# Later due times for DMAs in a planner, a wider gate, and two more DMA transposes, in a recurrence followed by a feed-forward stage

## The chip, the cores and the metric

The kernel runs on one core of a Trainium2 chip. The metric is device time in microseconds (us) of one execution. Three executions of the kernel before were timed: 184.87, 186.39 and 186.94 us, median 186.39 us. A fourth one was profiled, and all readings of the trace are from it.

## The reference

```python
# q, k, v, alpha: (B=4, H=8, S=768, D=48) float32; w_in 384x2048, w_out 2048x384
for t in range(S):
    state = alpha[:, :, t, :, None] * state + einsum('bhd,bhe->bhde', k[:, :, t], v[:, :, t])
    y[:, :, t] = einsum('bhd,bhde->bhe', q[:, :, t], state)
x = y.transpose(0, 2, 1, 3).reshape(B * S, H * D)        # 3072 tokens of 384
out = (relu(x @ w_in) ** 2) @ w_out                      # 3072 x 384
```

A gated linear recurrence (the "GLA part") makes x, and a feed-forward stage (the "MoE part", in the kernel's names m1 for `x @ w_in` and m2 for the product with `w_out`) makes the output from it.

## The kernel before, in words

The 3072 tokens are cut into 24 chunks of 128 tokens, numbered 0 to 23, six to a batch entry. A chunk passes through the GLA part like this. Four loads of 192 KB (`at` for alpha, `qt`, `kt`, `vt`; `add_load`, issued at L371 on SyncE's queue) bring it in. ScalarE takes the logarithm of alpha (L396, tile `L_s`); TensorE sums the logarithms over the tokens (`p0`, and `pT` in transposed form); ScalarE exponentiates the sums. From chunk 11 on (`RAW`) q and k are cast to bf16 on GpSimd (L413, tile `rawb`) and transposed by DMA (L416, tile `rawt`, two per chunk), and VectorE multiplies them with the transposed exponentials (L507 for q, L510 for k, both into tile `qkT`). TensorE makes the scores (tile `sc`), VectorE masks them (L561), TensorE adds both parts of y, and ScalarE casts y to bf16 (L386, tile `xn`). Last, xn is transposed into `xT_big`, the right operand of m1. Before the change, chunks 18 to 22 do this by a DMA transpose on SyncE's queue (L620); the others by three TensorE transposes (issued by a helper, so their line is L243) into a PSUM bank and a copy on VectorE (L388).

The MoE part takes the chunks in 12 groups: group 0 is chunks 0 to 3, groups 1 and 2 are one chunk each, and groups 3 to 11 two each (group 7 is chunks 14 and 15, group 8 is 16 and 17, group 9 is 18 and 19). m1 of a group needs x of all its chunks. It writes three PSUM banks in turn; ScalarE applies the relu out of them (L676, tile `r`), VectorE squares (L684, tile `gT`), and m2 of the group follows. All matmuls are issued by one helper, so they share line L240 and are told apart by their tiles.

The order of the work is made by a planner in the kernel's own Python (`Plan`, `Op`). Every operation is added with an engine, an estimated duration, an added latency `lat` until its result may be used, and a priority. `run` plays the program through on paper, engine by engine, and sorts all operations by their planned start; they are emitted in that order, and each engine and DMA queue of the chip then works through its own list in order, waiting where a semaphore says so. A planned figure therefore costs no time by itself: it moves an operation up or down in the list of its engine. The lists that matter here:

- "DMA" (loads) and "TR" (DMA transposes) both end up in SyncE's one queue. A load has duration `LD1` = 1.0 and `lat` 2.4 from chunk 6 on, so its data are planned for 3.4 us after its planned start. A transpose of q or k has duration `TLD` = 1.0 and `lat` `TLAT` = 4.0, so 5.0 us, and its place in the list is set 2.0 us later (`TLATE`, through the field `late`). The DMA transpose of xn has 0.8 + 4.0 us and `late` 1.0.
- A gate holds back TensorE's first operation of a chunk in the GLA part: chunk s may start when s <= LEAD + (MoE work planned so far) / 5.12, where a chunk's MoE work is 5.12 planned us, and LEAD is 3.7.

```python
            op.start = t + getattr(op, "late", 0.0)
            ...
            op.done = t + op.dur + op.lat
            ...
        self.order.sort(key=lambda o: o.start)
```

Of the kernel before, what the change touches and what calls it, by code (L numbers as in the profile page):

```python
# [141 lines left out]
def kernel(  # L142
# [93 lines left out]
    def pin(ins):  # L236
        tc.keep_in_program_order(ins)
# [4 lines left out]
    def tr(*a):  # L242
        pin(nc.tensor.transpose(*a))  # L243
# [14 lines left out]
    X_SLACK = 0.2  # L258
    LD = 0.98
    LD1 = 1.0  # L260
    WLD = 2.1
    LAG = 3.2
    SQ_PRIO = 0.0

    def add(eng, dur, emit, *deps, **kw):
        return plan.add(Op(eng, dur, emit, deps, **kw))
# [6 lines left out]
    def load_w(which):  # L273
# [25 lines left out]
        prev = w_cast[-SB] if len(w_cast) >= SB else None  # L299
        ld = add("DMA", WLD * n / 4 + 0.03, e_issue, prev, lat=LAG if which == "o" else 2.0)  # L300
        op = add({"POOL": 0.1 + 0.46 * n, "DVE": 0.1 + 0.2 * n, "ACT": 0.1 + 0.32 * n}, 0, e_cast, ld, prio=-3.0)
# [8 lines left out]
    SRC = dict(srcs)  # L310
    EARLY = 4
    RAW = 11
    XTURN = (18, 23)
    TLD, TLAT, TLATE = 1.0, 4.0, 2.0
    NR = 3
    R = {}

# [46 lines left out]
    def add_load(s, nm):  # L364
        d = C[s]
        b, c = divmod(s, NCH)

        def ld():
            if nm not in d:
                d[nm] = loads.tile([P, H, D], FP32, name=nm)  # L370
            pin(nc.sync.dma_start(out=d[nm], in_=SRC[nm][b, c]))  # L371
        prev = C[s - LB].get("use_" + nm) if s >= LB else None
        d["ld_" + nm] = add("DMA", LD if s < 4 else LD1, ld, prev, lat=2.0 if s < 4 else LAG if s < 6 else 2.4, at=0.6)

    def add_chunk(s):
        d = C[s]
# [189 lines left out]
        if not last:  # L566
# [7 lines left out]
            prev = C[s - 1].get("sb") if s else None  # L574
            if c == 0 and s:
                prev = C[s - 2]["sb"]
# [37 lines left out]
        def e_p4():  # L614
            d["px"] = psum(p4, [P, KT, P], BF16)
            for j in range(KT):
                tr(d["px"][:, j, :], d["xn"][:, j * P:(j + 1) * P], ident_bf)
        if XTURN[0] <= s < XTURN[1]:
            def e_xt():
                pin(nc.sync.dma_start_transpose(out=xT_big[:, :, s * P:(s + 1) * P], in_=d["xn"]))  # L620
            d["x"] = add("TR", 0.8, e_xt, xn, lat=TLAT)
            d["x"].late = 1.0
            d["end"] = xn
            return
        p4 = plan.add(Op("PE", 0.165, e_p4, [xn], takes=GLA_BANKS, lat=0.14, **g))
# [159 lines left out]
    for d in DMA_ORDER + list(range(6, NT)):  # L785
        if d in ("i", "o"):
            load_w(d)
        elif d == "at":
            add_joint_alpha()
        elif isinstance(d, tuple):  # L790
            add_load(*d)
            if d[0] >= JN:
                if all("ld_" + nm in C[d[0]] for nm, _ in srcs):
                    add_chunk(d[0])
            elif d == JLAST:
                for s in range(JN):
                    add_chunk(s)
        else:
            for nm, _ in srcs:
                if nm != "at":  # L800
                    add_load(d, nm)
                elif d <= 9:
                    add_load(d, nm)
                if nm == "at" and 9 <= d < NT - 1:
                    add_load(d + 1, nm)
            add_chunk(d)
# [24 lines left out]
                b2 = add_last(g, tt, b2, pools) if GT[g] + tt == NT - 1 else add_moe2(g, tt, b2, {}, range(NQ), pools)  # L831
        sq[(g, "free")] = b2

    LEAD = 3.7

    def gate(op):
        s = getattr(op, "gla", None)
        if s is not None:
            return s <= LEAD + (prog["m1"] + prog["m2"]) / 5.12
        return True  # L840
# [60 lines left out]
```

## Time and profile before

| What | Value |
|---|---|
| median of three runs (lowest, highest) | 186.39 us (184.87, 186.94) |
| the profiled execution: its own time | 185.07 us |
| its span, from the first to the last instruction | 183.4 us |
| mean granted TensorE clock | 1.000 |
| busy: PE (TensorE) | 177.5 us, 97% of the span |
| busy: DVE (VectorE), ACT (ScalarE), POOL (GpSimd) | 127.1, 126.5, 39.4 us |
| DMA issues on SyncE's queue that are transposes | 26 of q and k, 5 of x |
| share of the 16 DMA engines taken by SyncE's queue (q1) | 80.7% |

PE is the matmul side of TensorE and PEld its weight loads, which overlap with it. A busy PE counts each matmul from its start to its end; matmuls are pipelined, so a second may start before the first has ended, and 97% busy is not 97% of what TensorE could do. The chain of waits follows the program back from its last instruction, at every step to what released it. SPq is SyncE's queue, which issues loads and DMA transposes and waits for nothing but their semaphores.

### The profile page before, as it was taken

Reading aid. Unit: us, or ns where it says so; the run is one execution under the profiler, and the core shown is the slowest. Engines: PE = TensorE matmul, PEld = TensorE weight load, DVE = VectorE, ACT = ScalarE, POOL = GpSimd, SP = SyncE. Lnnn points to the kernel's source line nnn. Section 1 sums busy time; section 2 is a strip of 40 time slices with the busy share of each in tenths; the row PEclk is TensorE's granted clock in tenths of the full one; section 3 lists DMA queues with packets and bytes.
Section 4 is the critical chain, followed back from the end, with each engine's and each line's share of the span. In section 5 each row is a group of like instructions: output and inputs, shape, how many; then the busy total and the mean of one; then the engine's idle time right before and its main releaser. Section 6 shows DMA issues by size and latency. Waiting matters only on the chain.

```text
span 183.4 us, 4946 instructions
## 1 busy us (share of the span) xinstructions
PE 177.5 (97%) x1908; PEld 130.5 (71%) x1908; DVE 127.1 (69%) x273; ACT 126.5 (69%) x286; POOL 39.4 (21%) x80
## 2 busy tenths in 40 slices
PE   7999999899999999999999998999999999999993
PEld 2577884567769877867768776667766777778663
DVE  1179898684999998778877867748855984744200
ACT  3677799226859996966967859847975895767321
POOL 8221100021131142132223133342323512000000
PEclk9999999999999999999999999999999999999999
DMA  5999999999999999998999599898898898901022
GB/s 168 215 212 252 302 366 321 326 220 204 177 191 201 194 179 173 141 190 161 150 193 202 113 240 186 161 227 162 170 201 182 176 163 194 301 13 43 12 77 86
DMA packets 120200, 34.12 MB, mean 186 GB/s; under 512 B 112400, under 2 KB 118928, under 8 KB 120176
## 3 DMA queue, kind: packets, MB, share of 16 engines
q1 hardware_dynamic: 119536, 31.83, 80.7%
q0 software_dynamic: 640, 1.97, 3.2%
q8 instruction: 15, 0.25, 0.6%
q14 instruction: 9, 0.07, 0.2%
HBM read 25.17 MB, written 4.72 MB: 163 GB/s over the span
## 4 chain that ended last, share of the span: by engine, by line
PE 49%; DMA 2%; ACT 1%; issue 0%; DVE 0%
PE bank L240 45%; DMA at<-in_alpha_dram 2%; PE sc L240 2%; PE st L240 1%; PE bank L243 1%; ACT aiT L454 0%; ACT r L676 0%; ACT ob L758 0%; ACT L_s L396 0%; ACT ob L716 0%; DVE xT_big L388 0%; ACT qkT L451 0%
## 5 line engine op out<-in xcount | busy, mean ns | idle before, releaser
L240 PE MATMUL bank<-xT_big,w_in_b 128*128 128x256 bf16 (+2 forms) x636 | 76.6, 262 | 0.9 <-ACT r L676 0.7
L240 PE MATMUL bank<-w_out_b,gT 128*128 128x384 bf16 (+1 forms) x400 | 71.6, 320 | 0.5 <-DVE w_out_b L296 0.5
L676 ACT ACTIVATE r<-bank 128x512 bf16<-128x512 f32 x96 | 56.6, 606 | 11.3 <-PE bank L240 9.9
L240 PEld LDWEIGHTS <-w_in_b 128*128 128x128 bf16 x636 | 52.7, 98 | 10.6 <-issue 1.5
L240 PEld LDWEIGHTS <-gT 128*128 128x128 bf16 x416 | 37.2, 98 | 18.7 <-DVE w_out_b L296 1.0
L684 DVE TENSOR_TENSOR gT<-r 128x512 bf16<-128x512 bf16 x96 | 41.8, 453 | 10.2 <-ACT r L676 9.0
L561 DVE TENSOR_TENSOR sm<-sc,utri_b 128x512 bf16<-128x512 f32 x48 | 30.8, 684 | 5.9 <-PE sc L240 5.7
L405 POOL CAST vb<-vt 128x384 bf16<-128x384 f32 x24 | 13.6, 569 | 69.1 <-DMA vt<-in_v_dram 55.2
L386 ACT CAST xn<-bank 128x384 bf16<-128x384 f32 x24 | 11.6, 482 | 11.6 <-PE bank L240 11.5
L505 DVE TENSOR_TENSOR kI_s<-kt,Ainv 128x384 bf16<-128x384 f32 x21 | 12.8, 611 | 7.8 <-ACT Ainv L466 7.8
L240 PEld LDWEIGHTS <-qkT 64*128 64x128 bf16 (+1 forms) x272 | 10.7, 95 | 6.4 <-issue 2.4
L586 ACT CAST sb<-st 128x384 bf16<-128x384 f32 x20 | 9.6, 482 | 7.7 <-DVE st L581 7.5
L758 ACT COPY ob<-bank 128x384 f32<-128x384 f32 x14 | 6.7, 480 | 8.0 <-PE bank L240 8.0
L396 ACT ACTIVATE L_s<-at 128x384 bf16<-128x384 f32 x20 | 10.5, 527 | 2.4 <-DMA at<-in_alpha_dram 2.3
L240 PE MATMUL bank<-warm 128*128 128x256 bf16 (+1 forms) x54 | 10.9, 348 | 1.3 <-DVE warm L188 1.3
L502 DVE TENSOR_TENSOR qA_s<-qt,A 128x384 bf16<-128x384 f32 x11 | 6.3, 575 | 8.0 <-ACT A L462 8.0
L413 POOL CAST rawb<-qt 128x384 bf16<-128x384 f32 x13 | 7.4, 570 | 20.3 <-DMA qt<-in_q_dram 20.3
L413 POOL CAST rawb<-kt 128x384 bf16<-128x384 f32 x13 | 7.6, 587 | 19.0 <-DMA kt<-in_k_dram 11.1
L581 DVE TENSOR_TENSOR st<-st,ae_s 128x384 f32<-128x384 f32 x20 | 11.1, 556 | 0.5 <-PE st L240 0.5
L466 ACT ACTIVATE Ainv<-bank 128x384 bf16<-128x384 f32 x21 | 10.5, 501 | 1.1 <-PE bank L240 1.0
L240 PE MATMUL sc<-qkT 64*128 64x128 bf16 x192 | 9.5, 219 | 0.0
L240 PEld LDWEIGHTS <-sm 128*128 128x128 bf16 x192 | 8.1, 96 | 1.7 <-issue 0.2
(64 smaller groups left out, 165.7 us busy)
## 6 DMA issues: line engine op xcount, KB each, us to landing
qt<-in_q_dram SPq DMA_DIRECT2D x24, 192.0 KB, 4.0
kt<-in_k_dram SPq DMA_DIRECT2D x24, 192.0 KB, 3.6
vt<-in_v_dram SPq DMA_DIRECT2D x24, 192.0 KB, 3.8
at<-in_alpha_dram SPq DMA_DIRECT2D x20, 192.0 KB, 4.0
wo<-in_moe_w_out_dram SPq DMA_DIRECT2D x4, 768.0 KB, 8.5
out_dram<-ob POOLq DMA_DIRECT2D x10, 192.0 KB, 3.1
wi<-in_moe_w_in_dram SPq DMA_DIRECT2D x4, 384.0 KB, 5.3
wi<-in_moe_w_in_dram SPq DMA_DIRECT2D x2, 768.0 KB, 8.3
```

The lines of the kernel that those rows point to most:

```text
L240: pin(nc.tensor.matmul(*a, **kw))
L386: pin(nc.scalar.copy(out_t, in_t))
L396: pin(nc.scalar.activation(L[:, :, 0:D], d["at"], AF.Ln))
L405: pin(nc.gpsimd.tensor_copy(d["vb"], d["vt"]))
L413: pin(nc.gpsimd.tensor_copy(R["b"][:, w, j, :, 0:D], d[nm]))
L466: pin(nc.scalar.activation(d["Ai"], d["pm"][:, 0:HD].rearrange("p (h d) -> p h d", h=H), AF.Exp, scale=-1.0))
L505: pin(nc.vector.tensor_mul(kI[:, :, 0:D], d["kt"], d["Ai"]))
L561: pin(nc.vector.tensor_mul(d["sm"][:, hh], d["sc"][:, hh], utri_b.to_broadcast([P, NP, P])))
L581: pin(nc.vector.tensor_mul(st4, st4, bcast(ae, D)))
L586: pin(nc.scalar.copy(d["sbt"], d["st"]))
L676: pin(nc.scalar.activation(box["r"][:, 0:w], box["ph"][:, 0:w], AF.Relu))
L684: pin(nc.vector.tensor_mul(gT[g][:, f0:f0 + per, lo * P:lo * P + n], r, r))
```

## The change

```diff
     LD1 = 1.0
+    LT = 4.2
     WLD = 2.1
...
-    XTURN = (18, 23)
-    TLD, TLAT, TLATE = 1.0, 4.0, 2.0
+    XTURN = (16, 23)
+    TLD, TLAT, TLATE, XLATE = 1.0, 6.0, 2.0, 2.6
...
-        d["ld_" + nm] = add("DMA", LD if s < 4 else LD1, ld, prev, lat=2.0 if s < 4 else LAG if s < 6 else 2.4, at=0.6)
+        d["ld_" + nm] = add("DMA", LD if s < 4 else LD1, ld, prev, lat=2.0 if s < 4 else LAG if s < 6 else 2.4 if s < RAW else LT + (1.0 if nm == "at" else 0.0), at=0.6)
...
-            d["x"].late = 1.0
+            d["x"].late = XLATE
...
-    LEAD = 3.7
+    LEAD = 4.1
```

In words: (1) loads of chunks 11 to 23 are planned to land 5.2 us after their planned start (`at`: 6.2) and not 3.4; (2) DMA transposes of q, k and x are planned to take 2 us longer; (3) the DMA transposes of x get a place in the list that is 1.6 us later than before; (4) chunks 16 and 17 use the DMA transpose for x as well, so their six TensorE transposes and two VectorE copies are gone; (5) the gate lets each chunk's GLA part begin 0.4 chunks of MoE work, 2.05 planned us, earlier. No instruction's size or operands change.

## The prediction

> **What bounds the kernel now.** I read the page first: its busy times and its slices.
>
> ```profile
> PE 177.5 (97%) x1908; PEld 130.5 (71%) x1908; DVE 127.1 (69%) x273; ACT 126.5 (69%) x286; POOL 39.4 (21%) x80
> ...
> DMA  5999999999999999998999599898898898901022
> ```
>
> TensorE is the bound, and in every slice up to 162 us the DMA engines are nearly as full. Next, the table of stretches says where TensorE has anything to give back.
>
> ```profile
> 57.00:104.00 47.00, 46.92 (x546) 36.76 (x543) 39.90 (x87) 38.53 (x91) 11.96 (x21) 1.00 0.94 170
> 104.00:112.00 8.00, 7.33 (x76) 5.32 (x75) 5.22 (x13) 5.48 (x13) 3.05 (x6) 1.00 1.00 208
> 112.00:163.00 51.00, 51.00 (x530) 37.59 (x529) 36.18 (x76) 38.10 (x88) 13.83 (x24) 1.00 0.86 186
> ```
>
> The columns are the stretch, its length, busy PE, PEld, DVE, ACT, POOL, the clock, the DMA share and GB/s. The figures of the change concern chunks 9 and later, so nothing moves before about 57 us; behind 163 us only m1 and m2 are left. Between them PE idles 0.08 + 0.67 + 0 us. One place holds nearly all of it, and the chain of waits names it:
>
> ```profile
> 105.28 4.13 DMA at<-in_alpha_dram
> 109.40 0.02 issue
> 109.42 0.34 ACT L_s L396
> ...
> 111.30 0.49 ACT r L676
> 111.79 0.04 issue
> 111.84 0.49 PE bank L240 x3
> ```
>
> The alpha load of chunk 19 takes 4.13 us where the planner allowed 3.4. ScalarE waits for it in order (0.71 us idle ahead of L_s), with an eviction, two exponentials and a relu queued behind; TensorE has filled its three m1 banks and waits for that relu. TensorE's own timeline gives the size:
>
> ```profile
> 108.89 2.29 PE L240 MATMUL bank<-xT_big,w_in_b 128*128 128x256 bf16 x18
> 111.84 0.49 PE L240 MATMUL bank<-xT_big,w_in_b 128*128 128x256 bf16 x3 [0.66 <-ACT r L676]
> ```
>
> Of such matmuls twelve in a row took 1.47 us with the last counted at its full 0.27, so one starts every (1.47 - 0.27) / 11 = 0.109 us. Eighteen need 1.96; the next group began 2.95 after the first. Lost: 0.99 us, 0.66 of it visible as idle.
>
> **Part 1, two chunks' x by DMA.** Gone are 2 x 3 TensorE transposes. The chain counts three of them in a row at 0.17 us (102.06, 162.04), so 0.34 us, all on the bounding engine. Gone too are two VectorE copies of 0.346 us; DVE is at 69%, so I count 0. Added are two issues on SyncE at 1.21 us (2.5 with the gaps) and their transfers (landing 2.3 to 5.2 us from issue, median 2.5). Loads behind them, those of chunks 20 and 21, come up to 2.5 us later; chunk 20's transposed k has lain 6.5 us before use and chunk 21's 4.8, so 0 here, and 0 to 0.4 us if parts 2 and 5 use that up as well. How late x comes is seen here (chunk 17, then chunk 18):
>
> ```profile
> 122.03 0.48 ACT L386 CAST xn<-bank 128x384 bf16<-128x384 f32 x1 [2.28 <-PE bank L240]
> ...
> 122.96 0.33 PE L243 MATMUL bank<-ident_bf,xn 128*128 128x128 bf16 x3
> ...
> 123.70 0.34 DVE L388 COPY xT_big<-bank 128x384 bf16<-128x384 bf16 x1
> ...
> 124.42 0.82 PE L240 MATMUL bank<-xT_big,w_in_b 128*128 128x256 bf16 x6
> ...
> 128.10 0.50 ACT L386 CAST xn<-bank 128x384 bf16<-128x384 f32 x1
> ...
> 130.92 1.21 SPq L620 DMA_TRANSPOSE xT_big<-xn  x1
> ```
>
> By TensorE, x of chunk 17 is there 2.0 us after its cast began (124.04 - 122.03), and m1 of group 8 starts 0.4 us later. By DMA, the five chunks 18 to 22 took 5.6 to 6.0 us from the cast's start to landing (128.10 to 133.87 the first). So x of group 8 comes 3.7 us later. What hides it: at 124.42 half of tile 13's m2 and all of tiles 14 and 15 are still to do, 40 matmuls at 0.161 us (eight took 1.46, the last of them 0.33) = 6.4 us, besides the GLA work between them. Cost 0 while that cover lasts; without it, up to 3.7 us.
>
> **Part 2, XLATE 2.6.** An x transpose stands 1.6 us lower on SyncE's list, behind one or two more issues (0.57 us a load, 1.2 to 1.9 a transpose). SyncE's own waits say what this is worth:
>
> ```profile
> SPq L416 <- POOL rawb L413: 11.1, 10, 1.7
> ...
> SPq L620 <- ACT r L676: 2.5, 1, 2.5
> SPq L620 <- ACT ob L758: 2.1, 2, 1.2
> ...
> SPq L620 <- ACT ae_s L458: 1.5, 2, 1.0
> ```
>
> (waiter, released by, us, times, longest). With L620 SyncE stood 6.1 us waiting for ScalarE while loads queued behind; the loads can take that time, x of a chunk pays 0 to 1.9 us. TensorE: between -0.2 and 0, I take 0.
>
> **Part 3, loads 1.8 us (alpha 2.8) later on paper.** Their readers move down the lists: L_s on ScalarE, the casts on GpSimd. Seen from issue, loads land after 2.9 to 5.3 us (median 3.6) in this stretch: the old 3.4 was short for half of them, 5.2 for hardly any. L_s of chunk 19 then stands 2.8 us lower, behind the relus that TensorE waited for, and its load has landed. Its first reader, p0 of chunk 19, ran at 128.17, 18 us later, so nothing is late in its place. Gain: the 0.99 us; bounds 0 (another in-order wait takes over) and 0.99 plus the other PE losses I find by spacing after 57 us, about 1 in pieces under 0.25. I take 0.99. GpSimd's 31.4 us of waiting for q and k loads only moves: POOL is busy 21%, and the output DMAs in its list (0.55 us each) have buffers for six.
>
> **Part 4, TLAT 6.** Transposes of q and k are planned for 7.0 us after their cast, not 5.0. In the trace the landing of chunks 12 to 18 came 4.5 to 7.6 us after the cast's end. VectorE's products and the scores move down TensorE's list. PEld waited for L510 six times, 1.6 us in all, behind running matmuls; between -0.4 and 0 on PE, I take 0.
>
> **Part 5, LEAD 4.1.** I counted the w_in and w_out matmuls ahead of each p0 in TensorE's order: 8.38 chunks' worth for chunk 12, 12.38 for chunk 16, 16.38 for chunk 20, against gates of 8.3, 12.3 and 16.3. So p0 sits on its gate, and the gate now opens 0.4 chunks earlier: at 6.77 us a chunk (scores of chunk 11 at 77.30, of chunk 23 at 158.54) that is 2.7 us. No work is added. It pays for part 1's later x (3.7 + up to 1.9 against 2.7) and for the later places of parts 3 and 4. Its price is slack at the transposed k: from its landing to L510 that reads it were 2.7 us at the least (chunk 14) and 6.5 at the most (chunks 19 and 20).
>
> **Sum.** 185.07 - 0.34 - 0.99 = 183.74 us against the profiled execution's own time, which is its span of 183.4 and 1.67 around it. The median of the three runs is 186.39, 1.32 above that execution. No trace shows where a 186.39 run spends it, so I leave it in: 186.39 - 1.33 = 185.06, forecast 185.1 us.
>
> **Rivals.** (B) Nothing but the 0.34 comes: the wait of chunk 19's load moves to another place, as ScalarE and SyncE still work in order and the DMA share at 104 to 112 us was 1.00. For it: L_s waited four times (2.3 us in all), and only once did TensorE feel it, so the place decides. Against: all loads from chunk 11 on get the allowance. 186.39 - 0.34 = 186.05 us.
>
> (C) More comes: the three runs spread over 2.07 us, more than all PE idle after 57 us, and if their excess is also late loads the change removes it. For it: four of the 13 alpha loads came late even in a quick run; against: nothing shown. 185.07 - 1.33 = 183.74 us, a time for the median too.
>
> (D) Slower: the transposed k becomes the wait. Consumers move up 2.7 us (part 5) while transposes slip behind two more loads (2 x 0.64 = 1.3, with the gaps). Chunk 14 has 2.7 us, so its scores would stand 1.3 us in TensorE's list; chunks 11 and 12 (3.0 and 2.8) likewise. A PE stall delays all later readers, so the largest counts, not the sum: 1.3, and 1.9 if three loads go ahead. It decides where the forward move plus the slip pass 2.7 us. Against it: the planner also holds the readers back to 7.0 us after the cast and only one landing in the list above was beyond that. 186.39 - 0.34 + 1.9 = 187.95 us with chunk 19's loss staying.
>
> (E) Slower: x of group 8 comes too late and m2 runs out. It needs x later by more than 6.4 us of m2 plus the GLA work; 3.7 + 1.9 - 2.7 = 2.9 is expected, so it takes 3.5 us more, as one x transpose whose transfer took 5.2 and not 2.5 us (chunk 22) shows to be possible only in part. Were the cover gone, 2.9 us: 186.39 + 2.9 - 0.34 = 188.95 us. By the Trainium skill, "VectorE: DVE Perf Modes", "Rules for kernel authors", a 128x128 transpose belongs on TensorE when PSUM can take the result, with DMA as the other choice; the trace agrees on the delay (2.0 against 5.6 to 6.0 us), but whether that delay reaches TensorE is what (E) decides.
>
> **How the numbers follow.** Forecast 0.44 (own range 184.2 to 185.8), B 0.23, C 0.16, D 0.11, E 0.06. The range leaves out the lower part of C and the ends of D and E: 183.5 to 187.9 us. About 1% (1.9 us) is what a measurement of this kernel can tell from no change, so the lines are at 184.5 and 188.3. Faster by over 1%: C, and about 0.16 of the forecast's lower end, 0.32. Slower by over 1%: E, and 0.07 for the upper end of D, together 0.13. Within: 0.55.
>
> **What would show it.** Right: chunk 19's L_s with no wait that TensorE feels, PE idle between 57 and 163 us under 0.4 us, 51 transposes of xn on L243 instead of 57, seven on L620; p0 of chunk 12 near 77.6 us; m1 of group 8 1 to 3 us later than 124.42 with no idle before it. Wrong: PE or PEld waiting on VectorE's L507 or L510 by more than 0.5 us at once (D), PE idle just ahead of group 8's m1 (E), or ScalarE's wait for an alpha load back at another chunk with TensorE idle behind it (B).

## The result and the profile after

The changed kernel is slower by 0.64%: the ratio to before is 1.0064, 95% interval 1.0035 to 1.0094. Over 22 runs of each, the medians are 186.25 us (184.79 to 189.01) and 185.70 us (183.61 to 187.79). Ratios, here and below, leave out runs more than 1.5% above the fastest of their kernel; medians have all runs, and where the two disagree both are given. The profiled execution of the changed kernel took 185.48 us with a span of 183.6 us, against 185.07 and 183.4 before. Both lie below their kernel's median, so the two traces show where time moved and not the whole difference.

The page of the changed kernel, the same lines:

```profile
PE 176.9 (96%) x1902; PEld 130.2 (71%) x1902; DVE 126.2 (69%) x269; ACT 126.5 (69%) x288; POOL 40.1 (22%) x80
...
DMA  5999899999999989989899898896898898920112
```

and its table of stretches:

```profile
57.00:104.00 47.00, 47.00 (x561) 37.26 (x559) 40.03 (x88) 39.08 (x94) 13.27 (x22) 1.00 0.96 178
104.00:112.00 8.00, 7.33 (x84) 5.54 (x83) 6.93 (x14) 5.87 (x16) 2.64 (x5) 1.00 1.04 210
112.00:163.00 51.00, 50.39 (x498) 36.32 (x497) 31.75 (x65) 35.69 (x83) 13.87 (x24) 1.00 0.86 187
```

Six TensorE instructions are gone, and PE idles 1.28 us between 57 and 163 us where it idled 0.75. Two of the prediction's signs came: p0 of chunk 12 runs at 77.38 us (80.28 before, 77.6 forecast), and m1 of group 8 starts at 127.38, 3.0 us later than before, with no idle time ahead of it. The alpha wait is gone as well, but two others stand in its place. TensorE's timeline at 108 and at 141 us:

```profile
107.93 0.33 PE L240 MATMUL st<-vb,kI_s 128*128 128x96 bf16 x4
108.93 0.40 PE L240 MATMUL sc<-qkT 64*128 64x128 bf16 x8 [0.67 <-DVE qkT L511]
...
140.00 0.81 PE L240 MATMUL bank<-w_out_b,gT 128*128 128x384 bf16 x4
141.43 0.81 PE L240 MATMUL bank<-xT_big,w_in_b 128*128 128x256 bf16 x6 [0.61 <-DMA xT_big<-xn]
```

First the scores of chunk 16 wait for the product with the transposed k (L511 here; lines after the first edit are one higher); then m1 of group 9 waits for x of chunk 19 by DMA. The first of these is not what the change costs: the kernel without x by DMA (below), which is level with before, has the same wait (0.67 us at 109.17). ScalarE's wait for alpha before (who, for whom, us, times, longest), and the tile view of alpha after:

```profile
ACT L_s L396 <- DMA at<-in_alpha_dram: 2.3, 4, 0.7
```

```profile
L397 ACT ACTIVATE L_s<-at x15: 514/522/546, 58.0 to 140.0; 128x384 bf16<-128x384 f32 x15
L372 SPq DMA_DIRECT2D at<-in_alpha_dram x13: 371/576/926, 58.2 to 134.3; - x13
its engine sat idle before it (us, times) until:
who waited for it (us, times):
```

Nothing is listed under "sat idle before it": ScalarE's 2.3 us of waiting for alpha are gone. The x transposes, five before and seven after:

```profile
L620 SPq DMA_TRANSPOSE xT_big<-xn x5: 1206/1210/1966, 130.9 to 155.1; - x5
...
DMA to landing us min/median/max: 2.3/2.5/5.2
```

```profile
L621 SPq DMA_TRANSPOSE xT_big<-xn x7: 1201/1811/2708, 115.5 to 155.5; - x7
...
DMA to landing us min/median/max: 2.3/4.0/5.8
```

An x transpose takes 4.0 us at the median from issue to landing, where it took 2.5, and its issue holds SyncE for 1.81 us and not 1.21. (With x by DMA alone, below, the landing takes 4.0 us too, but the issue stays at 1.21.)

### The profile page after: what moved, and what is told of

The parts are those of the page before. It is cut to its first block, busy times and chain, and to the rows that moved or that the text cites. A ratio compares the mean times of both kernels' runs of the same rounds, so it can differ in the third digit from the quotient of the medians.

```text
span 183.6 us, 4935 instructions
## 1 busy us (share of the span) xinstructions
PE 176.9 (96%) x1902; PEld 130.2 (71%) x1902; DVE 126.2 (69%) x269; ACT 126.5 (69%) x288; POOL 40.1 (22%) x80
## 4 chain that ended last, share of the span: by engine, by line
PE 79%; DMA 8%; ACT 6%; DVE 4%; issue 1%; ACTq 0%; DVEq 0%; SPq 0%
PE bank L240 70%; DMA wi<-in_moe_w_in_dram 5%; PE bank L243 4%; PE sc L240 4%; ACT r L677 4%; DMA xT_big<-xn 3%; PE st L240 1%; DVE qkT L508 1%; DVE sm L562 1%; ACT Ainv L467 1%; DVE gT L685 1%; DVE w_in_b L297 1%; DVE w_out_b L297 0%; ACT xn L387 0%; ACT qkT L452 0%
## 5 line engine op out<-in xcount | busy, mean ns | idle before, releaser
L240 PE MATMUL bank<-xT_big,w_in_b 128*128 128x256 bf16 (+2 forms) x636 | 75.2, 262 | 0.7 <-DMA xT_big<-xn 0.6
L685 DVE TENSOR_TENSOR gT<-r 128x512 bf16<-128x512 bf16 x96 | 41.1, 444 | 15.8 <-ACT r L677 14.8
L414 POOL CAST rawb<-kt 128x384 bf16<-128x384 f32 x13 | 8.2, 634 | 11.9 <-DMA kt<-in_k_dram 11.9
L773 POOL DMA_DIRECT2D out_dram<-ob x10 | 5.6, 556 | 19.6 <-ACT ob L759 14.9
```

What stands on the lines that cost most here:

```text
L240: pin(nc.tensor.matmul(*a, **kw))
L414: pin(nc.gpsimd.tensor_copy(R["b"][:, w, j, :, 0:D], d[nm]))
L685: pin(nc.vector.tensor_mul(gT[g][:, f0:f0 + per, lo * P:lo * P + n], r, r))
```

## The experiments

Theory X: x of chunks 16 and 17 by DMA is the loss, either because x comes late (X-late) or because two more transposes load SyncE's queue and the DMA engines (X-load). Theory L: the wider gate is the loss. Theory P: the later planned landings and places are.

| kernel | ratio to before, 95% interval | median us (before's beside it) |
|---|---|---|
| whole change | 1.0064 (1.0035 to 1.0094) | 186.25 (185.70) |
| x by DMA alone | 1.0058 (1.0010 to 1.0106) | 186.71 (185.87) |
| whole without x by DMA | 1.0007 (0.9967 to 1.0047) | 185.53 (185.87) |
| LEAD alone | 1.0088 (1.0048 to 1.0129) | 187.25 (185.87) |
| whole without LEAD | 1.0117 (1.0032 to 1.0201) | 189.39 (185.87) |
| alpha's landing alone | 1.0023 (0.9980 to 1.0066) | 185.46 (185.85) |
| later landings and places alone | 1.0021 (0.9988 to 1.0053) | 186.06 (185.85) |
| no x by DMA at all | 1.0050 (1.0011 to 1.0089) | 186.51 (185.85) |
| two transposes into scratch, planned | 1.0136 (1.0074 to 1.0198) | 188.81 (185.85) |
| x planned late, on TensorE | 1.0033 (0.9990 to 1.0077) | 186.14 (185.91) |
| x by DMA moved to other chunks | 1.0045 (1.0003 to 1.0086) | 186.46 (185.91) |
| alpha's landing and LEAD 3.9 | 1.0078 (1.0041 to 1.0116) | 187.14 (185.91) |
| x by DMA alone, group 9 later | 0.9993 (0.9929 to 1.0057) | 187.21 (185.93) |
| whole, group 9 later | 1.0101 (1.0034 to 1.0167) | 187.35 (185.93) |
| alpha's landing, group 9 later | 1.0003 (0.9960 to 1.0045) | 185.42 (185.93) |
| two transposes into scratch, outside the plan | 1.0064 (1.0019 to 1.0109) | 187.40 (185.83) |
| five of them | 1.0300 (1.0223 to 1.0376) | 192.74 (185.83) |

**Part by part.** Each of x and LEAD was done alone and left out.

```diff
 # x by DMA alone, on the kernel before         # whole without x: XTURN = (18, 23)
-    XTURN = (18, 23)
+    XTURN = (16, 23)
 # LEAD alone, on the kernel before             # whole without LEAD: LEAD = 3.7
-    LEAD = 3.7
+    LEAD = 4.1
```

> The kernel before with one edit: x of chunks 16 and 17 by DMA (XTURN 16). The whole change measured 1.0064 of before, about +1.2 us. Theory X (the two chunks' x by DMA lands 3.7 us later, loads SyncE's queue, and m1 of groups 8 and 9 waits for it): about +1.2 us, ratio 1.004 to 1.008. Theory L (the wider gate puts readers of DMA data too early in TensorE's order): -0.3 us, the six transposes gone, ratio 0.998. Theory P (the later planned landings and places push x back): -0.3 us as well.

> The changed kernel with x of chunks 16 and 17 back on TensorE (XTURN 18). Theory X: the loss is gone, 1.000 of before or a little less. Theories L and P: the loss stays, ratio 1.006 to 1.009 (the 0.34 us of transposes come back on top).

> The kernel before with LEAD 4.1 alone. Theory L: +1.2 us, ratio 1.005 to 1.008, with TensorE waiting on VectorE's product with the transposed k (L511) in the trace. Theories X and P: no loss, 0.997 to 1.002; by the prediction's reading a little less than before, since a wider gate pays for late data.

> The changed kernel with LEAD back at 3.7. Theory L: the loss is gone, ratio 0.998 to 1.002. Theory X: the loss grows, since the gate no longer pays for the later x: 1.008 to 1.02. Theory P: it grows too, 1.008 to 1.02. If the parts are independent and small, 1.006.

X by DMA costs 0.58% alone, and without it the rest of the change stands level with before: theory X holds both ways. LEAD costs 0.88% alone, yet taking it out of the whole does not bring the time back: theory L holds for the old landings and falls for the new ones. (Whether the whole is worse without LEAD is not shown: the median is 3.1 us higher, but the two intervals overlap.) ScalarE's wait for alpha with LEAD alone:

```profile
ACT L_s L397 <- DMA at<-in_alpha_dram: 8.6, 8, 2.2
```

ScalarE waits 8.6 us for alpha where before it waited 2.3, as chunks are asked for earlier and alpha is still planned too soon. TensorE idles 2.99 us between 57 and 163 us in that execution (188.88 us, above that kernel's median), and its two longest waits, 0.86 us at 73.22 and 1.18 us at 113.10, follow back along the chain to an alpha load. It is not the whole of LEAD's cost: with alpha's landing planned later and a gate of 3.9 the kernel still measures 1.0078 (below).

**Landings alone, no x by DMA, scratch.** One edit sets alpha's `lat` to 5.2 for chunks 11 to 23 and nothing else; one sets LT, TLAT and XLATE alone; one sets `XTURN = (23, 23)`; one adds, to the kernel before, planned DMA transposes into a tile that nobody reads:

```diff
+        if s in (16, 17):
+            def e_sx():
+                pin(nc.sync.dma_start_transpose(out=scr[:, :, (s - 16) * P:(s - 15) * P], in_=d["xn"]))
+            add("TR", 0.8, e_sx, xn, lat=TLAT).late = XLATE
```

> The kernel before with one edit: alpha's loads of chunks 11 to 23 are planned to land 6.2 us after their start. Theory A (the prediction's part 3: ScalarE's in-order wait for alpha is what TensorE lost): ScalarE's wait for alpha falls from 2.3 us to about 0 and the time by up to 1 us, ratio 0.994 to 0.998. Rival (another in-order wait takes over at once): the wait falls too, the time stays, 0.998 to 1.003.

> The later planned landings and places alone (LT, TLAT, XLATE), with LEAD 3.7 and x of chunks 16 and 17 on TensorE. If the parts add up (whole change 1.006, without the lead 1.012, x about 0.006): 1.004 to 1.008, with TensorE waiting in front of m1 for x that the plan puts later. If the later landings are free and only x cost in the run without the lead: 0.997 to 1.002.

> The kernel before with no x by DMA at all: chunks 18 to 22 go back to TensorE, 15 transposes more, 0.85 us of TensorE by the prediction's price. If x by DMA costs more than it saves for every chunk, as theory X-load has it: faster than before, 0.985 to 0.998. If only the place matters (X-late; before has no wait for these five): slower by the 0.85 us, 1.003 to 1.007.

> The kernel before, with x of chunks 16 and 17 still transposed on TensorE, and a DMA transpose of the same two xn tiles into a scratch tile besides, which nobody reads (extra work, not less). Theory X-load (the two transposes cost by loading SyncE's queue and the DMA engines): about the loss of the first experiment, ratio 1.004 to 1.009. Theory X-late (they cost because m1 waits for x that comes later): 0.998 to 1.003.

> A second profile of the two transposes into scratch. If its loss is the edit's: again 187 us or more and TensorE waiting for a transposed k near 153 us. If the wait there was an accident: a loss spread over other places.

With alpha's landing alone, ScalarE's wait fell from 2.3 to 0.3 us and no gain could be measured; in its trace TensorE idles 0.69 us elsewhere, ahead of group 9:

```profile
142.10 0.50 PE L240 MATMUL bank<-xT_big,w_in_b 128*128 128x256 bf16 x3 [0.69 <-DMA xT_big<-xn]
```

All landings and places together, without LEAD and x, are level too. Without any x by DMA the kernel is slower by 0.5%, near the 0.85 us priced for 15 transposes: for chunks 18 to 22 the DMA path pays, so X-load is not true of every chunk. The planned scratch run measures more than x by DMA itself, though the intervals overlap. (In the scratch kernels line numbers are two to four higher than before.) In its first profile TensorE waited 2.58 us at 155.7 us for L512, the product with the transposed k of chunk 22, which had landed 0.1 us before the product began; in the trace of before this k lay 5.0 us. The second profile took 186.05 us and had this wait at the same place:

```profile
150.24 1.46 PE L241 MATMUL bank<-w_out_b,gT 128*128 128x384 bf16 x8
152.38 0.40 PE L241 MATMUL sc<-qkT 64*128 64x128 bf16 x8 [0.68 <-DVE qkT L512]
```

So the wait comes with the edit, and its length changes from execution to execution.

**Late or load.** The second profile of x by DMA alone (185.76 us), at group 9 again:

```profile
139.97 0.36 PE L240 MATMUL bank<-vb,sm 128*128 128x48 bf16 x8
141.34 0.50 PE L240 MATMUL bank<-xT_big,w_in_b 128*128 128x256 bf16 x3 [1.00 <-DMA xT_big<-xn]
```

```diff
 # x planned late, on TensorE: XWAIT = 4.1 planned us behind the copy's duration, 3.7 later than before
-            deps = [C[s]["x"] for s in ...]
+            deps = [(C[s]["x"], XWAIT if s in (16, 17) else None) for s in ...]
 # x by DMA moved
-        if XTURN[0] <= s < XTURN[1]:
+        if s in (16, 17, 20, 21, 22):
 # group 9 later: on x by DMA alone, on the whole change, on alpha's landing alone
-            d["x"] = add("TR", 0.8, e_xt, xn, lat=TLAT)
+            d["x"] = add("TR", 0.8, e_xt, xn, lat=TLAT + (1.5 if s in (18, 19) else 0.0))
```

> A second profile of x of chunks 16 and 17 by DMA alone. If the wait ahead of m1 of group 9 is what the edit costs, it is there again with about 1 us of idle TensorE; if it was one execution's accident, the lost time sits elsewhere in this profile.

> The kernel before with one edit in the planner: m1 may use x of chunks 16 and 17 only 3.7 planned us later than it is there, about what the DMA path costs on paper. x stays on TensorE, no DMA is added. Theory X-late (the order with a later m1 of group 8 is what costs): the loss of x by DMA without its saving, 1.006 to 1.009. Theory X-load (the two more transposes in SyncE's queue and on the DMA engines cost): no loss, 0.997 to 1.002.

> The kernel before with five x by DMA as before, but of chunks 16, 17, 20, 21 and 22, and those of 18 and 19 on TensorE. Theory X-load by count: as many DMA transposes as before, so 0.997 to 1.003. X-load by place (a transpose costs where loads of four more chunks still come behind it): 1.003 to 1.008. X-late at group 9 (TensorE waits only for x of chunk 19): no wait for x ahead of group 9, 0.996 to 1.001.

> The kernel before with alpha planned to land 6.2 us after its start and LEAD 3.9, no other part of the change. If the wider gate hurts alone only because alpha then comes late: 0.993 to 1.000, a candidate faster than both kernels. If the wider gate costs by other waits too: 1.002 to 1.008.

> x of chunks 16 and 17 by DMA alone, with x of chunks 18 and 19 planned to land 1.5 us later, so that m2 work stands ahead of m1 of group 9. If the wait ahead of group 9 is the loss (1.0058): no such wait in the trace, about 1 us less, ratio 0.998 to 1.002. If the two transposes cost by load on SyncE's queue and the DMA engines: the wait goes but the loss stays, 1.004 to 1.008.

> The whole change with the same edit: x of chunks 18 and 19 planned 1.5 us later still. If the wait ahead of group 9 (0.61 us idle in its profile) is the loss: 1.000 to 1.004. If load is: 1.005 to 1.008.

> Alpha planned to land 6.2 us after its start, LEAD 3.7, x of chunks 16 and 17 on TensorE, and x of chunks 18 and 19 planned 1.5 us later. Its predecessor without the last edit had 0.69 us idle ahead of group 9 and a median of 185.46 us. If both in-order waits are the loss that can be had back: 0.992 to 0.998, faster than both kernels. If the waits move again: 0.998 to 1.003.

The wait ahead of group 9 repeats (1.07 and 1.00 us): x of chunk 19 took 5.1 and 5.2 us from issue to landing, where it took 2.4 before. Planned away, the wait goes, and the loss does not: in the whole change the ratio stays at 1.0101, and the trace (of an execution of 189.41 us) has 1.9 us of TensorE waiting for L511 in three places instead. On x by DMA alone that edit is undecided (ratio 0.9993, but the median is 1.3 us above before's). x planned late is undecided as well (1.0033 lies between both theories), and moving two of the five DMA transposes to earlier chunks measures 1.0045, as X-load by place has it, with an interval (from 1.0003) that does not exclude X-load by count. Alpha's landing with a gate of 3.9 was to be a faster kernel and is not: x of chunk 19 was waited for 1.84 us. Alpha's landing with the old gate and group 9 later was to be faster as well and is level. No version is shown to beat the kernel before.

The last two runs took the planner out. They issue the transposes into scratch from inside the emission of the VectorE copy, so the lists of the compute engines are those of before (in the traces these engines run the same instructions in the same order, and SyncE's list differs by the added issues alone):

```diff
             cast(xT, xT_big[:, :, s * P:(s + 1) * P], d["px"])
+            if 16 <= s < 18:      # the second run: 13 <= s < 18
+                pin(nc.sync.dma_start_transpose(out=scr[...], in_=d["xn"]))
```

> The kernel before, its order on TensorE, VectorE, ScalarE and GpSimd unchanged, with two DMA transposes of xn into a scratch tile (chunks 16 and 17) on SyncE's queue that no plan knows of: extra work, nothing left out. Theory load: 1.004 to 1.009, with TensorE waiting for a transposed k or an x behind them. Theory order (what costs is that the planner reshuffles everything): 0.998 to 1.003.

> The same with five such transposes, of chunks 13 to 17. Theory load: two and a half times the first run's loss, 1.010 to 1.025. Theory order: 0.998 to 1.005.

Theory order falls, X-load stands: 1.0064 for two, 1.0300 for five, which is more than load was expected to cost (1.010 to 1.025). The first one's trace is of an execution of 188.93 us, above that kernel's median. TensorE waits 0.73 us for the scores of chunk 20. The product named there, L512, needs the transposed k, but this k had landed at 133.09, 6.5 us before L512 began. The chain of waits leads to another load, alpha of chunk 23:

```profile
134.01 3.64 DMA at<-in_alpha_dram
...
138.56 0.51 ACT qkT L453
...
139.09 0.43 DVE qkT L509
...
139.60 0.44 DVE qkT L512
140.04 0.05 issue
140.09 0.40 PE sc L241 x8
```

ScalarE waits for this alpha in order, with the exponentials of chunk 20 (L453) queued behind it. It already did so in the trace of before; the first line is from there, the second from the run with two transposes outside the plan:

```profile
136.42 0.52 ACT L396 ACTIVATE L_s<-at 128x384 bf16<-128x384 f32 x1 [0.46 <-DMA at<-in_alpha_dram]
...
137.67 0.52 ACT L398 ACTIVATE L_s<-at 128x384 bf16<-128x384 f32 x1 [1.26 <-DMA at<-in_alpha_dram]
```

ScalarE's wait is 0.80 us longer. The second wait of TensorE is for x of chunk 21, issued at 155.08 where before issued it at 151.71:

```profile
157.78 0.49 PE L241 MATMUL bank<-xT_big,w_in_b 128*128 128x256 bf16 x3 [2.13 <-DMA xT_big<-xn]
```

SyncE's list has hardly a gap, and an added transpose (1.21 and 1.79 us) takes the place of two or three loads:

```profile
117.18 0.58 SPq L373 DMA_DIRECT2D kt<-in_k_dram  x1
117.85 1.21 SPq L632 DMA_TRANSPOSE scr<-xn  x1
119.11 0.57 SPq L373 DMA_DIRECT2D vt<-in_v_dram  x1
119.74 0.57 SPq L373 DMA_DIRECT2D at<-in_alpha_dram  x1
120.35 0.89 SPq L373 DMA_DIRECT2D qt<-in_q_dram  x1
```

Just behind the second one the list stood 2.8 us behind that of before. A part of this was made up, but alpha of chunk 23 was still issued 1.21 us late (first line before, second line this run), while TensorE was only 0.45 us late (scores of chunk 19 at 132.40 and 131.95):

```profile
132.80 0.58 SPq L371 DMA_DIRECT2D at<-in_alpha_dram  x1
...
134.01 0.68 SPq L373 DMA_DIRECT2D at<-in_alpha_dram  x1
```

With five transposes the same load stops TensorE at the same scores. It is issued at 135.52 and lands at 140.66, while the transposed k of these scores had landed at 134.76:

```profile
140.69 0.52 ACT L398 ACTIVATE L_s<-at 128x384 bf16<-128x384 f32 x1 [3.94 <-DMA at<-in_alpha_dram]
...
143.27 0.61 PE L241 MATMUL sc<-qkT 64*128 64x128 bf16 x8 [3.57 <-DVE qkT L512]
```

## Why the prediction was wrong, point by point

- **Part 1 failed, by its load.** The prediction priced the two transposes' load on what stands behind them at 0, with 0 to 0.4 us as the bound, because the transposed k of chunks 20 and 21 had 6.5 and 4.8 us of slack. Two transposes outside the plan cost 1.0064, about 1.2 us at 185.83; x by DMA alone cost 1.0058, 1.1 us, with the 0.34 us of TensorE saved inside it. The slack was read for the transposed k alone, but the same list carries the alpha loads and x. Alpha of chunk 23 had no slack at all: ScalarE waited 0.46 us for it in the trace of before. SyncE's list had hardly a gap and the DMA engines were nearly full (share 0.86 to 1.00), so the delay was worked off only in part; about 0.8 us of it stood at that alpha load. TensorE, whose list is fixed, met it at the tightest places. In the profiles of the whole change, of x by DMA alone and of the scratch runs these were alpha of chunk 23, x of chunks 19 and 21 and the k of chunk 22, but not the k of chunks 20 and 21 that had been priced.
- **Part 3 was right in its mechanism and not in its gain.** ScalarE's wait for alpha went as said, in the whole change (2.3 to 0) and alone (2.3 to 0.3). The 0.99 us did not come: alone 1.0023 (0.9980 to 1.0066). That is rival B's way: the trace has other waits in its place (0.33 us at 110.81, 0.69 us ahead of group 9).
- **Part 5, "no work is added", was half wrong.** LEAD alone costs 0.88%. Together with the later landings it costs nothing that can be measured: later landings without LEAD measure 1.0021, LEAD without them 1.0088, both without x 1.0007. The prediction added the parts as if independent; these two are not.
- **Parts 2 and 4** were taken at 0, and the landings and places together (1.0021, 0.9988 to 1.0053) do not contradict that. XLATE by itself was not run. The 6.1 us that part 2 read as SyncE waiting are not shown to be waiting: four of the five x transposes started within 0.1 us of the end of the issue ahead and took 1.21 to 1.23 us, though the view counts waits of 0.5 to 1.2 us for them. By the same count it is 7.1 us in seven after. Of the landings that part 4 read, two and not one (rival D's count) came more than 7.0 us after their cast's end: 7.2 and 7.7 us, both of chunk 14.
- **Rival D** named the right sort of wait (L511, 0.67 us at 108.93) for another reason. The transposed k of chunk 16 had landed at 105.22; the product started late because VectorE's product ahead of it took 1.34 us where its median is 0.42 in the trace of before. What stretched it was not tried; the kernel without x by DMA has the same product (1.34 us) and the same wait, and is level with before. **Rival E** named the wrong group: x of group 8 was covered, as the prediction said, and group 9's was not. The rule of the Trainium skill named there ("VectorE: DVE Perf Modes", "Rules for kernel authors") does better than the prediction for chunks 16 and 17 and worse for 18 to 22, where giving all transposes back to TensorE costs 0.50%.
- **The baseline.** The median of three runs (186.39) is 0.69 us above that of 22 (185.70). That moved the forecast, not its sign. The changed kernel's median of 186.25 us lies inside the range of 183.5 to 187.9 us by luck: the range was wide and began from a high baseline, while the gain of 1.33 us in the sum did not come.

What stays open: how the load's cost splits between SyncE's issue time and the DMA engines' time was not tried. In the trace with two transposes outside the plan alpha of chunk 23 took as long from issue to landing as before (3.64 and 3.60 us), so its lateness came from its issue; the DMA transposes of q and k took 3.9 us at the median and not 3.4 (112 to 150 us). And x coming late (X-late) by itself may cost up to 0.8% (interval of x planned late).

## What to carry to other kernels

When a queue is full, price an added transfer by the tightest of all the transfers behind it, not by the slack of one kind of them: look for those that an engine already waits for. Better, put the same transfer into the kernel with its result unused, outside any plan, and measure it. With fixed instruction orders, removing the wait that a profile shows may be worth nothing until the next wait behind it is known. A wait names the instruction that ended last; follow the chain to the transfer behind it before you name the cause. And a planner's parameters are to be tried in pairs: a wider gate was a loss with the old landings and none with the new.

## What the runs showed of the hardware

A long wait of TensorE costs twice. With five transposes in scratch it idled 3.57 us, and the clock column (behind POOL's count) falls after it:

```profile
139.00:143.30 4.30, 0.73 (x7) 0.23 (x6) 1.01 (x2) 2.56 (x7) 1.32 (x3) 0.87 1.11 141
143.30:150.00 6.70, 6.70 (x50) 4.50 (x51) 2.48 (x5) 2.23 (x5) 2.06 (x4) 0.57 0.90 183
150.00:170.00 20.00, 20.00 (x211) 15.20 (x209) 14.22 (x32) 15.30 (x34) 2.03 (x4) 1.00 0.61 154
```

At 0.57 the 6.70 us did the work of about 3.8 (an estimate, 0.57 x 6.70). Waits of 2.58 us (scratch, planned) and 2.13 us (outside the plan) left it at 1.00. The Trainium skill, "TensorE: Matmul & The Clock Gate", section "Why this matters for your kernels", asks for no idle gap above about 3 us; these three waits agree. One run does not: in the whole change with group 9 later, three waits of 0.50, 0.90 and 0.33 us within 3 us were followed by a mean clock of 0.76 from 153 to 160 us. There the clock fell with no single wait above 0.9 us near it.

DMAs in flight can be held up together. In both profiles of x by DMA alone, a 16 KB packet of the queue that the page calls instruction (q8) starts at 136.5 and 137.4 us, and the load of chunk 22's q, issued at 132.9 and 133.3, lands after 5.7 and 5.9 us, where the loads ahead of it took 3.4 to 3.8. It is this stretch in which x of chunk 19 took 5.1 and 5.2 us. The trace of the whole change has the same: a packet at 137.5, and alpha of chunk 23, q of chunk 22 and x of chunk 19, issued from 134.3 to 136.2, land after 5.2 to 5.8 us. In the trace of before such a packet at 136.4 held up nothing that can be seen. That the packet is the cause is not shown.
